# An edge MLP with gather and scatter on one core: transposes a period ahead, chunks scattered in pairs by adding DMAs

## The chip, the cores and the metric

The kernel runs on one core of a Trainium2 chip. The metric is the device time in microseconds of one execution; times given for a kernel are medians over runs. The engines are TensorE (PE; PEld are its weight loads), VectorE (DVE), ScalarE (ACT), GpSimd (POOL) and SyncE (SP, which issues DMAs).

## The reference

A message-passing layer on a graph of 12,500 nodes and 800,000 edges. Each edge takes the features of its two ends (64 each) and its own attributes (16), multiplies them by `w_msg` (144 x 64), and passes the result through SiLU. The messages are summed over the edges that end at each node, and each node is updated.

```python
N, deg, D, De = 12500, 64, 64, 16          # E = N * deg = 800000, src and dst random
m_in  = jnp.concatenate([x[src], x[dst], e_attr], axis=-1)
msg   = silu(m_in @ w_msg)
agg   = segment_sum(msg, dst, N)
out   = silu(jnp.concatenate([x, agg], axis=-1) @ w_upd)
```

## The kernel before

**Two halves that run at the same time.** The first half sorts edges by destination; the second computes messages from the sorted edges. Nodes are cut into 128 buckets of 98. The product with `w_msg` is split: `A_d` in memory holds each node's part for `src`, and `BW` on chip holds, for each bucket, the part for `dst` and the rows for the attributes.

*Sorting, by steps.* A step takes 8 tiles of 128 edges (782 steps in all). `Step.onehot` (ACT) writes each edge's bucket as a one-hot row `hf`; `sums` (DVE) and `count` (PE, into `z`) count how many edges of the same bucket stand before each edge; `ranks` (DVE) reduces that to a rank; `expand` (DVE) compares the ranks with a ramp (`ioS`, held in PSUM) to get `hit`, and multiplies the edges' records (16 attributes and one packed index, `R` = 17 floats) into their slots, `X`; `move` (PE) multiplies `hf` by `X`, so that in `pl` each bucket (a partition) gets its records side by side. What is collected before it is written out is a *chunk*: 8 tiles for the first 140 steps, 12 tiles after that. So in the first stage every step ends a chunk, and after that three steps end two. `end.blk` (ACT) copies a chunk out of PSUM, `place` (DVE) works out where each bucket's records go in the store `st` in memory, and `scatter` (POOL) is an indirect DMA with one row for each bucket: up to 30 records of 68 B, 2040 B. A record that does not fit in its chunk's limit is noted in `LOST` and handled at the end.

*Messages, by batches.* The store is read back in tiles of 128 records of one bucket. A `Group` (up to 64 tiles) forms over several periods: it works out on DVE and PE which buckets have whole tiles ready, and SP loads those tiles into `rt`. Groups take units of 1 tile first (`FIRST`), then of 2, then of 4 tiles (`QU`). A `Batch` is 6 or 8 tiles of a group. `gather` (POOL) issues one indirect DMA a tile, which fetches 128 rows of `A_d` (256 B each); `onehot` (DVE, ACT) builds `q`, the one-hot of the node within the bucket beside the attributes; `transpose(0)` (PE) and `transpose(1)` (ACT) turn it into `qt`; `product` (PE) multiplies by `BW`, into `pre`; `message` adds the gathered rows (DVE) and applies SiLU (ACT); `reduce` (PE) multiplies by the one-hot and sums by node, into `ag`; `add` (DVE) adds that to `ACC`.

**The order of the work.** It is written out by hand in `period`. One period carries a step in three stages (`h`, then `z`, then `p`) and a batch in four (`q`, `t`, `a`, `r`), each one period behind the one before. Every engine executes in the order in which `period` issues. Before the change PE's order within a period is: `count` of z, `transpose` of t, `reduce` of r, `move(0)` of p, `product` of t, `move(1)` of p. (`move(1)` is the second part of a step in which one 12-tile chunk ends and the next begins.) POOL's order is: half of the batch's gathers, the scatter of the chunk that ended a period earlier, the other half. A batch's first gather also waits for the reduction of the batch four earlier, whose buffer it reuses.

**The planner.** `step` decides before each period whether a new group may start. It does not know the data: `Draws` draws 16 sets of Poisson counts, and a group starts when its units would be there in all 16, with 6 to spare. Stages follow one another: a stage of larger units begins when the stage before has taken its total.

**PSUM tiles** come from pools of one buffer each: `z`, `cb` (constants), `pl`, `t` (transposes), `pre` and `ag`; the small matmuls of a forming group use `ag` too.

**After the last step** come the remaining batches, the last partial tiles and the node update.

Of the kernel before, what the change touches and what calls it, by code (L numbers as in the profile page):

```python
# [3 lines left out]
F32 = mybir.dt.float32  # L4
# [25 lines left out]
XR = 2 + W  # L30
# [6 lines left out]
FIRST = [(1, 48, BT, (1, 0, 1, 0)), (2, 24, 6, (3, 3, 2, 2))]  # L37
# [7 lines left out]
SUMMED = "the sum that this reads waits for the gathers into its buffer, the older ones there were read ahead of them"  # L45
LISTED = "the work list holds buckets and tiles of the store"


def mpnn_kernel(tc, x, e_attr, src, dst, w_msg, w_upd, out):
# [7 lines left out]
    CAPT = (K8 * S8 + (NCH - K8) * S) // P + 2  # L57
# [3 lines left out]
    NREC = TOP * P  # L61
# [11 lines left out]
    with es:  # L73
# [4 lines left out]
        pz = pool("pz", 1, space=PSUM)  # L78
        pc = pool("pc", 1, space=PSUM)
        pp = pool("pp", 1, space=PSUM)  # L80
        pt = pool("pt", 1, space=PSUM)
        ppre = pool("ppre", 1, space=PSUM)
        pag = pool("pag", 1, space=PSUM)

        A_d = dr.tile([NB * BK, D], F32, name="A_d")
        XU_d = dr.tile([BK, NBK * D], F32, name="XU_d")
        st = dr.tile([NREC, R], F32, name="st")
        st_t = st.rearrange("(t e) c -> t (e c)", e=P)

# [32 lines left out]
        cb = pc.tile([P, 512], F32, name="cb")  # L122
        ioB = cb[:, 0:BK]
        ioS = cb[:, BK:BK + S]
        hit = cb[:, P:P + M * S].rearrange("p (k s) -> p k s", s=S)
# [3 lines left out]
        nc.vector.tensor_scalar(out=ioS, in0=iof[:, 0:S], scalar1=RK, scalar2=None, op0=OP.add)  # L129

# [7 lines left out]
        ub = {u: cp.tile([NBK, 1], F32, name=f"ub{u}") for u in (1, 2, QU)}  # L138
        nc.vector.tensor_scalar(out=ub[1], in0=ipf, scalar1=float(CAPT), scalar2=None, op0=OP.mult)
        ptr0 = cp.tile([NBK, 1], I32, name="ptr0")  # L140
        nc.vector.tensor_scalar(out=ptr0, in0=ub[1], scalar1=float(P), scalar2=None, op0=OP.mult)
# [3 lines left out]
        capm = cp.tile([NBK, 2 + len(FIRST)], F32, name="capm")  # L145
# [8 lines left out]
        stages = []  # L154
        for i, (u, gt, bt, give) in enumerate(FIRST):
# [7 lines left out]
            stages.append(dict(u=u, gt=gt, bt=bt, cap=cap, caps=caps, total=u * sum(caps)))  # L163
        stages.append(dict(u=QU, gt=GT, bt=BT, cap=None, caps=None, total=None))
# [5 lines left out]
        class Nodes:  # L170
# [20 lines left out]
            def turn(t):  # L191

                xt_p = pt.tile([P, BT * P], F32, name="xt_p", tag="t")
# [9 lines left out]
            def parts(t, i):  # L203
                ps = (ppre, pag)[i % 2].tile([P, 512], F32, name="abp", tag=("pre", "ag")[i % 2])
# [8 lines left out]
        def tables():  # L213
# [3 lines left out]
            for i in range(-3, len(ts) + 2):  # L217
                if at(i):
                    at(i).turn()
# [117 lines left out]
        ACCf = ACC.rearrange("p b k -> p (b k)")  # L337
        for t in X:
            nc.gpsimd.memset(t[:, :, 0:1], 1.0)
        nc.gpsimd.memset(sent, 0.0)  # L340
# [6 lines left out]
        def later():  # L347
# [5 lines left out]
            if len(zeros) == 15:  # L353
                for k in range(P // SR):
# [7 lines left out]
        bp = pool("bp", 2)  # L362
        sm = pool("sm", 4)
        rcp = pool("rcp", 2)
# [6 lines left out]
        state = dict(x=0, rt=0, u=1, ptr=ptr0, done=done0, stage=0, taken=0, straight=True)  # L371

        blocks = []
        gathers = []
        live = []

        prior = dict(step=None, pl=None)

        class Step:


            def __init__(c, hi, rec, index, n=M):

                c.hi, c.rec, c.n = hi, rec, n
# [4 lines left out]

                c.last = {k: K8 + (index * M + k) // c.size for k in range(n) if c.pos[k] == c.size - 1}  # L390
# [27 lines left out]
            def count(c):  # L418

                hb = c.hf.bitcast(BF16).rearrange("p m (b two) -> p m b two", two=2)[:, :, :, 1]  # L420
                c.z = pz.tile([P, M, NBK], F32, name="z")
# [13 lines left out]
            def expand(c, rs=None):  # L435
# [6 lines left out]
                nc.vector.tensor_tensor(out=c.x[:, :, 1], in0=rank, in1=limc[:, c.turn, :], op=OP.is_ge)  # L442
                nc.vector.tensor_tensor(out=hit, in0=ioS[:, None, :].to_broadcast([P, M, S]), in1=rank[:, :, None].to_broadcast([P, M, S]), op=OP.is_equal)
                for k in range(0, c.n, 2):
                    n = LIM[c.pos[k]]
                    nc.vector.tensor_tensor(out=c.x[:, k:k + 2, 2:2 + n * R].rearrange("p k (s c) -> p k s c", c=R), in0=hit[:, k:k + 2, 0:n, None].to_broadcast([P, 2, n, R]),  # L446
                                            in1=c.rec[:, k:k + 2, None, :].to_broadcast([P, 2, n, R]), op=OP.mult)

            def move(c, part=None):
# [4 lines left out]
                for k in reversed(range(c.n)) if whole else range(c.n):  # L454
# [3 lines left out]
                    if n == (c.size - 1 if whole else 0):  # L458
                        prior["pl"] = pp.tile([P, 512], F32, name="pl")
                    pl = prior["pl"]  # L460
                    w = 2 + LIM[n] * R
                    ends = n == (0 if whole else c.size - 1)
                    nc.tensor.matmul(pl[:, 0:w], c.hf[:, k, :], c.x[:, k, 0:w], start=(n == (c.size - 1 if whole else 0)), stop=ends, skip_group_check=True)  # L463
                    if ends:
                        w = 2 + LIM[c.size - 1] * R
                        end = Chunk(*c.last.values())
                        end.blk = bp.tile([NBK, XR], F32, name="blk")[:, 0:w]
                        nc.scalar.activation(end.blk, pl[:, 0:w], AF.Copy)  # L468
                return end

        class Chunk:


            def __init__(c, index):
                c.index, c.m = index, M if index < K8 else min(C, NT - K8 * M - (index - K8) * C)

            def place(c, ptr_new):

                c.ptr, b = state["ptr"], c.blk
                lost = LOST[:, c.index:c.index + 1]  # L480
                nc.vector.scalar_tensor_tensor(out=lost, in0=b[:, 1:2], scalar=0.0, in1=b[:, 0:1], op0=OP.is_gt, op1=OP.mult)
                nc.vector.scalar_tensor_tensor(out=ptr_new, in0=b[:, 0:1], scalar=lost, in1=c.ptr, op0=OP.subtract, op1=OP.add)
                state["ptr"] = ptr_new

            def scatter(c):
                i = nc.gpsimd.indirect_dma_start(out=st, out_offset=bass.IndirectOffsetOnAxis(ap=c.ptr, axis=0), in_=c.blk[:, 2:], in_offset=None)  # L486
                tc.declare_no_dep(i.ins, group="units", reason=WHOLE)
                blocks.append(i.ins)

        def regs(row, u, n, engine, top):  # L490
            return nc.values_load_multi_w_load_instructions(row[0:1, u:u + n], engines=(engine,), min_val=0, max_val=top, skip_runtime_bounds_check_because=LISTED)[1]

        class Group:


            def __init__(g, u, ptr, done_old, done_new, ceil, gt=GT, base=None, cap=None, bt=BT):
                g.u, g.ptr, g.done_old, g.done_new, g.ceil, g.gt = u, ptr, done_old, done_new, ceil, gt
                g.base = ub[u] if base is None else base
                g.b0, g.cap = None, cap
                g.gu, g.bt = gt // u, bt  # L500
                g.quick = cap is not None
                g.nl = NL[u]
# [32 lines left out]
            def fourth(g):  # L535
                k = g.k
                gu = g.gu
                if k == 0:
                    urec = g.u * P
                    c = (urec - 1) / (2.0 * urec) * (1.0 if g.ceil else -1.0)  # L540
# [8 lines left out]
                    nc.vector.scalar_tensor_tensor(out=new, in0=v, scalar=-MAGIC, in1=g.done_old, op0=OP.add, op1=OP.subtract)  # L549
                    nc.vector.tensor_tensor(out=t1, in0=g.base, in1=g.done_old, op=OP.add)  # L550
# [26 lines left out]
            def middle(g):  # L577
# [4 lines left out]
                elif g.k == 1:  # L582
                    cbc, mat = g.wl[7], g.mat
                    g.ps = pag.tile([P, 512], F32, name="ps2", tag="ag")
# [10 lines left out]
        class Last(Group):  # L595


            def __init__(g, b0, n):
                super().__init__(1, ptrg, None, None, False, n)
# [11 lines left out]
            def middle(g):  # L611
                if g.k == 1:
                    g.ps = pag.tile([P, 512], F32, name="ps3", tag="ag")
# [6 lines left out]
        class Batch:  # L620
# [41 lines left out]
            def transpose(t, step):  # L662
                w = t.n * P
                if step == 0:
                    t.grp.over = t.i0 + t.n >= t.grp.gt
                    t.tq = pt.tile([P, BT * P], F32, name="tq", tag="t")
                    for j in range(t.n):
                        nc.tensor.transpose(t.tq[0:KQ, j * P:(j + 1) * P], t.q[:, j, :], ident)  # L668
                else:
                    t.qt = qtp.tile([KQ, BT * P], F32, name="qt")  # L670
                    nc.scalar.activation(t.qt[:, 0:w], t.tq[0:KQ, 0:w], AF.Copy)  # L671

            def product(t):
                t.pre = ppre.tile([P, 512], F32, name="pre")
# [16 lines left out]
            def reduce(t):  # L691
                t.ag = pag.tile([P, 512], F32, name="ag")
                u = t.grp.u
                for j in range(0, t.n // u, 2):
                    for k in range(u):
                        for v in range(j, min(j + 2, t.n // u)):
                            i = v * u + k
                            o = nc.tensor.matmul(t.ag[t.half(v), v // 2 * BK:(v // 2 + 1) * BK], t.g[:, i, :], t.q[:, i, 0:BK], start=(k == 0), stop=(k == u - 1))  # L698
                            t.gathers.append(o.ins)
# [13 lines left out]
        pipe = dict(h=None, z=None, s=None, q=None, t=None, a=None)  # L713

        def period(step=None, batch=None, ptr_new=None):

            h, z, p, s = step, pipe["h"], pipe["z"], pipe["s"]
            q, t, a, r = batch, pipe["q"], pipe["t"], pipe["a"]
            forms = [g for g in work["forming"] if not g.ready()]
            e = None  # L720
            pipe.update(h=h, z=z, q=q, t=t, a=a)
# [15 lines left out]
            for g in quick:  # L737
                g.middle()
                g.k = 1
            if t:  # L740
                t.transpose(0)
                t.weights()
                t.transpose(1)
            if r:
                r.reduce()
            if z:
                z.ranks()
            if a:
                a.message()
            if r:  # L750
                r.add()
# [7 lines left out]
            for g in quick:  # L759
# [427 lines left out]
```

## Time and profile before

| | us |
|---|---|
| median of 3 runs | 8911.29 |
| lowest, highest | 8909.55, 8912.29 |
| span of the profiled execution | 10886.0 |

The profiled execution is one run under the hardware profiler; it is longer than the timed runs. Its times are from the start of its span. In rows of groups the columns are: line, engine, operation, output and input tiles, count; then busy us and mean ns of one; then idle us just before them and what ended that. In rows of a timeline: start us, length us, engine, line, operation, tiles and shape; in brackets the engine's idle time before it and what ended it. `issue` is idle time in which the engine waited for nothing that the profile shows, `remote` is a release that the profile can't name. In rows of stretches: the stretch and its length, then busy us and count of PE, PEld, DVE, ACT and POOL, the granted PE clock as a share of full speed, the share of DMA engines, GB/s.

| stage | us from the start |
|---|---|
| steps alone | 0 to 200 |
| first gather | 200.12 |
| last step's rank | 10036.79 |
| last gather | 10848.35 |

### The profile page before, as it was taken

To read this page: it belongs to the slowest core of one execution; us is meant where nothing else is said; L and a number is where in the kernel's file an instruction comes from. 1 tells how busy PE (TensorE), PEld (TensorE's weight loads), DVE (VectorE), ACT (ScalarE), POOL (GpSimd) and SP (SyncE) were. 2 spreads that over 40 slices of the span, in tenths; PEclk is the share of its full clock that TensorE was granted. 3 is DMA by queue.
4 is the path that set the end of the run, shared out by engine and by line. 5 is a ranking of instruction groups with operands and counts; after the bars stand their busy time and mean duration, and the time that the engine had idled before them with its cause. 6 is when DMAs were issued, how large, how long until landed. Compare 5 with 4: busy or idle time off the path is not lost. (4 is left out here: it accounts for less than half of the span.)

```text
span 10886.0 us, 155616 instructions
## 1 busy us (share of the span) xinstructions
PE 8949.9 (82%) x49053; PEld 6219.2 (57%) x49816; DVE 7231.4 (66%) x15936; ACT 5082.6 (47%) x12594; POOL 6571.4 (60%) x6908
## 2 busy tenths in 40 slices
PE   8788888888888888888888888888888888888556
PEld 5566655555555555555555555555555555555555
DVE  7777776666666666766666666666666666766232
ACT  6455554444444444444444444444444444544211
POOL 2565666666666666666666666666666666666555
PEclk9999998999989988999998999999899998988555
DMA  3111111111111111111111111111111111111212
GB/s 97 44 49 48 49 49 46 43 47 42 47 42 46 45 44 45 44 43 44 46 43 46 44 44 43 46 47 43 45 42 46 43 47 44 44 45 41 46 36 44
DMA packets 662903, 501.15 MB, mean 46 GB/s; under 512 B 492983, under 2 KB 529911, under 8 KB 662071
## 3 DMA queue, kind: packets, MB, share of 16 engines
q0 software_dynamic: 238976, 349.72, 12.3%
q1 hardware_dynamic: 422775, 141.27, 5.9%
q8 instruction: 400, 6.55, 0.3%
q14 instruction: 432, 3.54, 0.1%
q10 hardware_dynamic: 320, 0.07, 0.0%
HBM read 330.05 MB, written 152.30 MB: 44 GB/s over the span
## 5 line engine op out<-in xcount | busy, mean ns | idle before, releaser
L649 POOL DMA_INDIRECT g<-A_d,sidx x6322 | 5997.6, 949 | 3658.7 <-issue 1620.7
L463 PE MATMUL pl<-X,hf 128*128 128x291 f32 (+5 forms) x12512 | 4745.0, 524 | 476.4 <-issue 428.3
L463 PEld LDWEIGHTS pl<-X,hf 128*128 128x128 f32 x12512 | 2538.7, 211 | 2159.4 <-issue 1737.4
L446 DVE TENSOR_TENSOR X<-cb,rec 128x442 f32<-128x442 f32 (+5 forms) x3128 | 2646.6, 908 | 26.7
L396 ACT ACTIVATE hf<-iof,shi 128x128 f32<-128x128 f32 x6256 | 1908.8, 389 | 1360.4 <-PE pl L463 449.0
L671 ACT ACTIVATE qt<-tq 114x1024 f32<-114x1024 f32 (+1 forms) x818 | 811.7, 992 | 2951.3 <-remote 2298.5
L433 DVE TENSOR_REDUCE rank<-z 128x8 f32<-128x1024 f32 x782 | 954.5, 1221 | 1270.3 <-remote 874.9
L677 PEld LDWEIGHTS pre<-w,qt 114*128 114x128 f32 x10496 | 1392.5, 209 | 687.8 <-ACT qt L671 467.1
L677 PE MATMUL pre<-w,qt 114*128 114x64 f32 x10496 | 1395.2, 291 | 345.6 <-ACT qt L671 317.6
L710 DVE TENSOR_TENSOR ACC<-ag,ACC 64x98 f32 x1938 | 496.7, 256 | 1553.3 <-remote 1131.7
L698 PE MATMUL ag<-q,g 128*64 128x98 f32 x12644 | 882.3, 276 | 490.4 <-remote 236.2
L698 PEld LDWEIGHTS ag<-q,g 128*64 128x64 f32 x12644 | 681.6, 151 | 668.8 <-issue 381.7
L668 PE MATMUL tq<-ident,q 128*114 128x128 f32 x6322 | 929.9, 294 | 103.3 <-issue 91.5
L668 PEld LDWEIGHTS tq<-ident,q 128*114 128x114 f32 x6322 | 812.6, 147 | 238.7 <-issue 122.6
L397 ACT ACTIVATE hf<-hf,ones 128x1024 f32<-128x1024 f32 x782 | 898.8, 1149 | 25.4
L486 POOL DMA_INDIRECT st<-blk,ptrs x567 | 567.2, 1000 | 561.4 <-ACT blk L468 272.2
L659 DVE TENSOR_TENSOR q<-cb,lo 128x784 f32<-128x784 f32 (+1 forms) x818 | 768.7, 940 | 96.1 <-PE ag L698 46.3
L468 ACT ACTIVATE blk<-pl 128x512 f32<-128x512 f32 (+1 forms) x568 | 324.9, 572 | 818.2 <-PE pl L463 500.9
L426 PE MATMUL z<-G,onesb 128*128 128x384 bf16 x1564 | 529.8, 339 | 78.9 <-issue 25.2
L682 ACT ACTIVATE g<-g 128x512 f32<-128x512 f32 (+1 forms) x818 | 498.4, 609 | 192.5 <-DVE g L681 111.8
L681 DVE TENSOR_TENSOR g<-pre,g 128x512 f32<-128x512 f32 (+1 forms) x818 | 541.3, 662 | 51.4 <-issue 37.2
L677 PE MATMUL pre<-BW,qt 114*128 (+1 forms) x2148 | 326.3, 314 | 99.0 <-ACT qt L671 64.8
(138 smaller groups left out, 5243.9 us busy)
## 6 DMA issues: line engine op xcount, KB each, us to landing
g<-A_d,sidx POOLq DMA_INDIRECT x6322
ea<-in_e_attr SPq DMA_DIRECT2D x260, 192.0 KB
rt<-st SPq DMA_DIRECT2D x1312, 34.0 KB
st<-blk,ptrs POOLq DMA_INDIRECT x567
rt<-st SPq DMA_DIRECT2D x434, 8.5 KB
nodes<-in_x SPq DMA_DIRECT2D x62, 98.0 KB
ACC<-rt SPq DMA_DIRECT2D x11, 544.0 KB
rt<-st SPq DMA_DIRECT2D x320, 17.0 KB
```

The costliest lines, as they stand in the source:

```text
L396: nc.scalar.activation(c.hf[:, k, :], iof, AF.Square, bias=c.hi[:, k:k + 1])
L397: nc.scalar.activation(c.hf, c.hf, AF.Relu, bias=ones, scale=-1.0)
L433: nc.vector.tensor_reduce(out=c.rank, in_=c.z, axis=AX.X, op=OP.max)
L446: nc.vector.tensor_tensor(out=c.x[:, k:k + 2, 2:2 + n * R].rearrange("p k (s c) -> p k s c", c=R), in0=hit[:, k:k + 2, 0:n, None].to_broad ...
L463: nc.tensor.matmul(pl[:, 0:w], c.hf[:, k, :], c.x[:, k, 0:w], start=(n == (c.size - 1 if whole else 0)), stop=ends, skip_group_check=True)
L486: i = nc.gpsimd.indirect_dma_start(out=st, out_offset=bass.IndirectOffsetOnAxis(ap=c.ptr, axis=0), in_=c.blk[:, 2:], in_offset=None)
L649: j = nc.gpsimd.indirect_dma_start(out=t.g[:, i, :], out_offset=None, in_=A_d, in_offset=bass.IndirectOffsetOnAxis(ap=t.grp.sidx[:, k:k + ...
L659: nc.vector.tensor_tensor(out=t.q[:, 0:n, 0:BK], in0=ioB[:, None, :].to_broadcast([P, n, BK]), in1=t.grp.lo[:, i0:i0 + n, None].to_broadca ...
L668: nc.tensor.transpose(t.tq[0:KQ, j * P:(j + 1) * P], t.q[:, j, :], ident)
L671: nc.scalar.activation(t.qt[:, 0:w], t.tq[0:KQ, 0:w], AF.Copy)
L677: nc.tensor.matmul(t.pre[:, i * D:(i + 1) * D], t.qt[:, i * P:(i + 1) * P], w, start=True, stop=True)
L698: o = nc.tensor.matmul(t.ag[t.half(v), v // 2 * BK:(v // 2 + 1) * BK], t.g[:, i, :], t.q[:, i, 0:BK], start=(k == 0), stop=(k == u - 1))
```

## The change

Five things are changed together.

1. *PSUM tiles are held for good.* They are allocated once and named (`zb`, `tb`, `plb`, `preb`, `agb`, `cb`). Small work lists of forming groups use a free corner of `agb` (`listing`).
2. *Transposes a period ahead.* `transpose(0)` of a batch moves from its second period (t) to the end of its first (q), behind `move(0)`. `message` moves ahead of `ranks`; `reduce` moves behind `move(0)`. PE's order is now: `count`, `move(0)`, `transpose` of q, `reduce`, `product`, `move(1)`. `reduce` gets one more matmul with a single column, after which the batch's buffer counts as read.
3. *A period more for chunks.* A chunk that ended is placed a period later (`e`) and scattered two periods later (`s`).
4. *Shared adding scatters.* In the 12-tile stage two chunks (428 chunks, 214 pairs) share one scatter. The first chunk's records stand at the right end of the first half of `BLK` and the second chunk's at the left end of the second half, so that in memory they follow one another; the rest of the row is zeros, and the DMA adds (`compute_op=OP.add`). Rows are 2 x 30 records, 4080 B. The ramp for right-aligned records, `ioD`, is held in SBUF. The store is filled with zeros beforehand: `fill` issues 271 DMAs on SP over the course of the kernel, each 128 rows of 4080 B from a block of zeros in memory, at least four ahead. `BLK` is one buffer of two halves, where `blk` had two buffers. In the 8-tile stage a scatter still writes one chunk without adding.
5. *Overlapping stages.* The first groups have 12, 12 and 24 tiles of one tile a unit, up to 2, 1, 2, 1 tiles a bucket by quarter (before: 48 tiles, up to 1, 0, 1, 0), in batches of 6 tiles (before: 8). Every stage keeps its own count of what it has taken, and `step` starts a group of the first stage that has enough. The large stage's first groups have 32 tiles instead of 64.

```diff
-FIRST = [(1, 48, BT, (1, 0, 1, 0)), (2, 24, 6, (3, 3, 2, 2))]
+FIRST = [(1, (12, 12, 24), 6, (2, 1, 2, 1)), (2, (24,), 6, (3, 3, 2, 2))]
+LATER = (32, 32, 32, GT)
...
+        def fill():
+            a = (P - S + len(filled) * ROW) * R
+            z = nc.sync.dma_start(st_b[:, a:a + ROW * R], Z_d)
+            filled.append(z.ins)
...
             def expand(c, rs=None):
-                nc.vector.tensor_tensor(out=hit, in0=ioS[:, None, :].to_broadcast([P, M, S]), in1=rank[:, :, None].to_broadcast([P, M, S]), op=OP.is_equal)
+                io = ioD[:, :, None, :].to_broadcast([P, 2, M // 2, S]) if turn else (ioS if c.right[0] else ioD[:, 0, :])[:, None, :].to_broadcast([P, M, S])
+                nc.vector.tensor_tensor(out=wide(hit), in0=io, in1=wide(rank[:, :, None].to_broadcast([P, M, S])), op=OP.is_equal)
...
+            def keep(c, pl, right):
+                if c.main:
+                    nc.scalar.activation(c.cnt[:, c.side, :], pl[:, f:f + 2], AF.Copy)
+                c.blk = BLK[:, c.side, 0:n]
+                nc.scalar.activation(c.blk, pl[:, a:a + n], AF.Copy)
...
             def scatter(c):
-                i = nc.gpsimd.indirect_dma_start(out=st, out_offset=bass.IndirectOffsetOnAxis(ap=c.ptr, axis=0), in_=c.blk[:, 2:], in_offset=None)
+                if c.single:
+                    i = nc.gpsimd.indirect_dma_start(out=st, out_offset=at, in_=c.blk, in_offset=None)
+                else:
+                    i = nc.gpsimd.indirect_dma_start(out=st, out_offset=at, in_=BLK.rearrange("p a w -> p (a w)"), in_offset=None, compute_op=OP.add)
...
             def reduce(t):
-                            o = nc.tensor.matmul(t.ag[t.half(v), v // 2 * BK:(v // 2 + 1) * BK], t.g[:, i, :], t.q[:, i, 0:BK], start=(k == 0), stop=(k == u - 1))
-                            t.gathers.append(o.ins)
+                            nc.tensor.matmul(t.ag[t.half(v), v // 2 * BK:(v // 2 + 1) * BK], t.g[:, i, :], t.q[:, i, 0:BK], start=(k == 0), stop=(k == u - 1))
+                o = nc.tensor.matmul(t.ag[0:t.n, 4 * BK:4 * BK + 1], t.g[:, 0:t.n, 0], ones, start=True, stop=True)
+                t.gathers.append(o.ins)
...
         def period(step=None, batch=None, ptr_new=None):
+            if e:
+                e.place(ptr_new)
             if t:
-                t.transpose(0)
                 t.weights()
                 t.transpose(1)
-            if r:
-                r.reduce()
+            if a:
+                a.message()
             if z:
                 z.ranks()
-            if a:
-                a.message()
-            if r:
-                r.add()
...
             if p:
-                e = p.move(0)
+                end = p.move(0)
+            if q:
+                q.transpose(0)
+            if r:
+                r.reduce()
             if t:
                 t.product()
             if p:
                 p.move(1)
-            if e:
-                e.place(ptr_new)
+            if r:
+                r.add()
...
-            pipe["s"] = e
+            pipe["e"] = end if end and end.whole else None
```

More of the change, by code (lines that the diff above doesn't have):

```diff
@@ L45 @@
 SUMMED = "the sum that this reads waits for the gathers into its buffer, the older ones there were read ahead of them"
+AHEAD = "the zeros are written ahead of the rows that any bucket can have reached; a scatter waits for those that it may reach"
 LISTED = "the work list holds buckets and tiles of the store"
@@ L388, in __init__ @@
                 c.prev, prior["step"] = prior["step"], c
+                c.right = [not main or c.turn == 2 or c.turn == 3 or (c.turn == 1 and k >= C - M) for k in range(M)]
                 c.last = {k: K8 + (index * M + k) // c.size for k in range(n) if c.pos[k] == c.size - 1}
@@ L464, in move @@
                     if ends:
[L465 to L468, printed above, removed]
+                        end = Chunk(*c.last.values(), c.main)
+                        end.keep(pl, c.right[k])
                 return end
         class Chunk:
-            def __init__(c, index):
-                c.index, c.m = index, M if index < K8 else min(C, NT - K8 * M - (index - K8) * C)
@@ L501, in __init__ @@
                 g.quick = cap is not None
+                g.back = state["back"]
                 g.nl = NL[u]
```

358 lines of the change are left out of this document (220 added, 138 removed).

## The prediction

> **What bounds the kernel now.** I read the page first (busy shares and costliest groups), then the clock by stage, then the timeline of GpSimd (POOL) alone, then who waited for whom.
>
> ```profile
> span 10886.0 us, 155616 instructions
> ...
> PE 8949.9 (82%) x49053; PEld 6219.2 (57%) x49816; DVE 7231.4 (66%) x15936; ACT 5082.6 (47%) x12594; POOL 6571.4 (60%) x6908
> ...
> L649 POOL DMA_INDIRECT g<-A_d,sidx x6322 | 5997.6, 949 | 3658.7 <-issue 1620.7
> L486 POOL DMA_INDIRECT st<-blk,ptrs x567 | 567.2, 1000 | 561.4 <-ACT blk L468 272.2
> ```
>
> By busy shares TensorE (PE, 82%) leads and POOL (60%) looks idle. POOL's timeline in the steady stage says otherwise:
>
> ```profile
> 5010.81 0.95 POOL L649 DMA_INDIRECT g<-A_d,sidx  x1 [2.44 <-remote]
> 5012.06 0.94 POOL L649 DMA_INDIRECT g<-A_d,sidx  x1 [0.30 <-issue]
> 5013.30 0.95 POOL L649 DMA_INDIRECT g<-A_d,sidx  x1 [0.31 <-issue]
> 5014.56 0.95 POOL L649 DMA_INDIRECT g<-A_d,sidx  x1 [0.30 <-DMA g<-A_d,sidx]
> 5015.81 1.00 POOL L486 DMA_INDIRECT st<-blk,ptrs  x1 [0.31 <-issue]
> 5017.11 0.96 POOL L649 DMA_INDIRECT g<-A_d,sidx  x1 [0.30 <-issue]
> ...
> 5020.88 0.94 POOL L649 DMA_INDIRECT g<-A_d,sidx  x1 [0.30 <-issue]
> 5024.34 0.95 POOL L649 DMA_INDIRECT g<-A_d,sidx  x1 [2.52 <-DVE g L681]
> ```
>
> Every indirect DMA is followed by 0.30 us in which POOL waits for nothing and still starts nothing. So a gather holds POOL 0.949 + 0.30 = **1.25 us** and a scatter 1.00 + 0.30 = **1.30 us**. All of them: 6322 x 1.25 + 568 x 1.30 = 7903 + 738 = **8641 us** (567 scatters in the row, and the first one, which has a row of its own).
>
> The rest of the profiled span, 10886 - 8641 = 2245 us, is mostly the 2.4 us ahead of each batch's first gather. That gather waits for the reduction of the batch four back. The trace shows why it comes late:
>
> ```profile
> 5005.52 0.38 PE L428 MATMUL z<-G,onesb 128*128 128x512 bf16 x1
> 5006.70 0.90 PE L698 MATMUL ag<-q,g 128*64 128x98 f32 x16
> 5010.14 1.23 DVE L433 TENSOR_REDUCE rank<-z 128x8 f32<-128x1024 f32 x1 [2.60 <-remote]
> ```
>
> PE's records put the end of z at 5005.90 and of the reduction at 5007.60, but the reader of z starts at 5010.14 and POOL's gather at 5010.81. PE's results are seen 3 to 4 us after their recorded end, in each such burst of short matmuls.
>
> The timed runs cannot contain this. Their median is 8911 us, 1975 below the profiled span, and POOL's slots alone take 8641 of it. The remaining 270 us are found at the two ends:
>
> ```profile
> 179.17 0.96 POOL L486 DMA_INDIRECT st<-blk,ptrs  x1 [5.66 <-ACT blk L468]
> 185.79 0.96 POOL L486 DMA_INDIRECT st<-blk,ptrs  x1 [5.66 <-ACT blk L468]
> 200.12 0.97 POOL L649 DMA_INDIRECT g<-A_d,sidx  x1 [13.37 <-DVE sidx L530]
> ...
> 238.44 0.95 POOL L649 DMA_INDIRECT g<-A_d,sidx  x1 [0.30 <-issue]
> 247.62 1.00 POOL L486 DMA_INDIRECT st<-blk,ptrs  x1 [8.23 <-ACT blk L468]
> ...
> 305.87 0.94 POOL L649 DMA_INDIRECT g<-A_d,sidx  x1 [0.30 <-issue]
> 311.27 1.00 POOL L486 DMA_INDIRECT st<-blk,ptrs  x1 [4.46 <-ACT blk L468]
> ...
> 343.56 0.96 POOL L486 DMA_INDIRECT st<-blk,ptrs  x1 [8.02 <-ACT blk L468]
> 355.12 0.98 POOL L649 DMA_INDIRECT g<-A_d,sidx  x1 [10.61 <-PE z L428]
> ...
> 10848.35 0.94 POOL L649 DMA_INDIRECT g<-A_d,sidx  x1 [0.30 <-issue]
> ```
>
> Before the first gather: 200, less 22 scatters of 1.30, is 171. Between the first stage of groups and the second (305.87 to 355.12, less one gather and four scatters): 43. At 238.44: 8. After the last gather: 36. Sum 258 of the 270. So I take it that in the timed runs **POOL's issue of indirect DMAs is the bound**, without a pause from the first group on. The profiled execution shows nothing around its span of 10886; I set the sum against that and against the median, in slots, not by a ratio.
>
> How far off is PE?
>
> ```profile
> L463 PE MATMUL pl<-X,hf x9628: 348/547/1207, 1702.1 to 9700.0; 128*128 128x223 f32 x36, 128*128 128x291 f32 x33, 128*128 128x359 f32 x32, 128*128 128x410 f32 x32
> 500.00:1300.00 800.00, 666.35 (x3726) 487.78 (x3799) 613.93 (x1613) 418.03 (x1028) 481.67 (x503) 0.92 0.20 49
> 1700.00:9700.00 8000.00, 6745.60 (x36911) 4577.32 (x37513) 5492.84 (x11580) 3859.84 (x9629) 4966.48 (x5216) 0.91 0.17 45
> 10100.00:10800.00 700.00, 425.53 (x2524) 372.08 (x2526) 185.68 (x495) 129.05 (x258) 417.93 (x443) 0.56 0.23 40
> ```
>
> The move makes 16 matmul records a step, so 1700 to 9700 holds 9628 / 16 = 602 periods. PE's busy time at the granted clock is 6745.60 x 0.91 / 602 = 10.2 us of full-clock work a period; VectorE (DVE) 9.1, ScalarE (ACT) 6.4. POOL, with eight gathers and two thirds of a scatter: 10.87. PE stands only 0.7 us behind.
>
> **The change, part by part.**
>
> *Shared adding scatters.* The 428 chunks behind the first 140 go out in pairs: 214 scatters fewer, 214 x 1.30 = **-278 us**. Each that is left moves rows of 4080 B instead of 2040 and adds in memory. No row shows an adding DMA. Nearest below: a gather of 256 B rows, 0.949; nearest above: two plain scatters, the work that it replaces, 2.60 with issue. From 256 B to 2040 B the price rises 0.05, so for twice the bytes I add 0.06, **+13 us** (ends -11 and +278). I take the low value because descriptors per row, not bytes, seem to set POOL's time, and their number stays 128.
>
> *Zero fill.* 271 DMAs of 128 rows go from memory to memory on SP's queue ahead of the scatters. SP issues them beside its loads of tiles; the DMA engines are 17% busy in the table above. Behind a fill on SP stand the loads of e_attr and of the next group's tiles, which run periods ahead. Price 0 in the steady stage. At the start the first scatters now wait for zeros, made on ACT, written out and copied: I take **+10 us** (0 to 20, against the 6.62 us between scatters at 179 and 185).
>
> *Overlapping stages, small first groups.* The first group asks for 12 tiles, not 48 of 64 buckets. A bucket gets about 8 records a step, so 12 (and 6 spare) full tiles of 128 exist near step 14.5, 54 near 17.4: three periods earlier. A 12-tile list loads in one period instead of three: two more. Placing a period later takes one back. Four periods of 6.62: **-26 us**. The later stages may start before the first ends, so the pauses of 43 and 8 go: **-51 us**. Batches of six tiles instead of eight (about 9 batches more) add no gathers.
>
> *Transposes ahead, message and reduce reordered, held PSUM tiles.* Product no longer waits within a period for transposes and ACT's copy. Both stand beside POOL's slots, so this is worth nothing while POOL binds; without that cover it is worth PE's waits, at most POOL's 10.87 less 10.2. The reduction now sits behind the first move and the new transposes on PE, so the next batch's first gather, and the seven and the scatter behind it, are released later in PE's period; their data is wanted two periods on, hence 0.
>
> *Closing matmul in reduce.* One 1-column matmul a batch, two records and two loads.
>
> ```profile
> L585 PE MATMUL ps<-mat,wl 128*1 128x16 f32 (+5 forms) x230 | 23.8, 179 | 17.7 <-DVE wl L562 5.9 <-DVE mat L561 4.0 <-remote 3.6
> L585 PEld LDWEIGHTS ps<-mat,wl 128*1 128x1 f32 x230 | 9.9, 81 | 42.0 <-issue 19.1 <-DVE wl L562 7.4 <-DVE mat L561 5.4
> L443 DVE TENSOR_TENSOR cb<-cb,rank 128x240 f32<-128x240 f32 x782 | 324.5, 415 | 3.0
> 5012.43 0.42 DVE L405 TENSOR_TENSOR G<-hf 128x256 bf16<-128x256 f32 x1
> ```
>
> At most 2 x (23.8 + 9.9) / 230 = 0.29 us; in a pipelined run, as the reduction's own 16 records in 0.90, 0.11. PE becomes 10.3 to 10.5 a period and POOL 8 x 1.25 + 1.36 / 3 = 10.45. They meet. For the 642 periods of the paired stage I take the upper end, 0.04 each: **+25 us** (0 to 25).
>
> *Place and keep.* Two more small ACT copies a pair, six small DVE operations instead of four, all beside POOL. But both halves of a pair share one buffer. The copy of the next pair's first half waits until the scatter has read it; behind that copy on ACT stand the next step's one-hots, and PE's second move waits for the freed bank. From POOL's start of that period: five slots (6.3), the landing, the copy (0.6), then PE's own work up to the reduction that frees POOL's same period of the next pair, about two of its 10.2 us periods: 27 plus the landing, against three POOL periods, 31.3. Price 0 while an adding scatter lands within 4 us.
>
> Sum: 8911 - 278 + 13 + 10 - 26 - 51 + 25 = **8604 us**, 3.4% less. Against the profiled execution the same terms give 10886 - 307 = 10579, if the 2.4 us stay.
>
> **Rivals.**
>
> *A, the adding scatter is dear.* If POOL builds twice the descriptors (it must read its target), each costs two plain slots and the saving is gone: 8604 + 278 - 13 = 8869. For it: read, add and write is more work; against: the flat price from 256 B to 2040 B. From 1.30 x 2 + 0.3 = 2.9 us it would end slower. 18 in 100.
>
> *B, slower: PE is the bound in the timed runs too.* Then POOL's fewer slots give nothing, and each of 818 batches pays for the closing matmul: 0.2 x 818 = 164, less the 67 at the start: 9008. It decides from 67 / 818 = 0.08 us a batch. For it: PE's 82%, 10.2 us close behind. Against: the 8641 + 258 that add up to the median. 12 in 100.
>
> *C, the shared buffer binds.* With a landing of 6 us, 2 us a pair: 8604 + 428 = 9030; at 5 us 8820. No row gives the landing of an adding scatter. 7 in 100.
>
> *D, VectorE locks POOL out.* In turns 0 and 1 the 'hit' compare (L443) reads its ramp from SBUF instead of PSUM, so both inputs lie in SBUF. If each held POOL for its 0.415 us, 428 of them cost 178: 8782. Against: the G sum of 5012.43 reads two SBUF inputs, lies across a gather, and that gather took 0.94. The Trainium skill (SBUF — State Buffer, Who interferes with whom) says that a VectorE instruction with two SBUF inputs contends with a GpSimd instruction that reads SBUF, which speaks against this change. By that rule it would be 8782; the trace does not agree for gathers. 5 in 100.
>
> **How the numbers follow.** Forecast 58, A 18, B 12, C 7, D 5 in 100. The likeliest gives 8604, its own range 8540 to 8680 (ends of the terms, and some jitter between PE and POOL now that they meet). To hold 8 in 10 the upper end must reach A: 8500 to 8890. A change under 0.2% (18 us) is about what this measurement cannot tell from none. Faster: 58 + 5, most of A (12) and part of C (3): 78. Same: 4, from A. Slower: B, and the rest of A and C: 18.
>
> **What would show it.** In the profile after: 214 adding scatters of about 1.06 us with 0.30 behind them (right), or 2 us and more (A). First gather near 175 to 185 instead of 200, no pause near 305. POOL again in runs of 1.25 us with one pause a batch. Gathers beside the compare at 0.95 (not D). ACT's copy of the first half waiting for a DMA or POOL would be C. If the time falls far less than POOL's slots do, the reading of POOL as the bound is wrong.

## The result and the profile after

The change makes the kernel slower: 9828.44 us (9827.24 to 9843.33) against 8910.91 (8909.55 to 8912.29), a ratio of 1.1034 [1.1018, 1.1049]. Forecast was 8604. The profile of before in the prediction shows an execution of 10886 us, and one chip met later takes 10868 for that kernel in every run; all kernels below were compared on chips where it takes 8910, except three that are marked.

The page of the changed kernel:

```profile
span 9825.4 us, 162309 instructions
...
PE 8600.8 (88%) x51528; PEld 6128.8 (62%) x51528; DVE 7362.0 (75%) x17005; ACT 5108.1 (52%) x13146; POOL 6564.7 (67%) x6696
```

Its gathers and its adding scatters on POOL (busy us and mean ns, then the idle time ahead of them):

```profile
L740 POOL DMA_INDIRECT g<-A_d,sidx x6322 | 6064.7, 959 | 2956.3 <-issue 1772.1 <-PE ag L790 947.3 <-DMA g<-A_d,sidx 125.7
L569 POOL DMA_INDIRECT st<-BLK,cnt x214 | 351.9, 1644 | 65.2 <-issue 53.6 <-ACT cnt L539 6.7 <-DMA g<-A_d,sidx 1.5
```

Two things are new. POOL's gathers now wait 947 us for the closing matmul of the reduction (L790). And an adding scatter takes 1.644 us, not the 1.06 that was forecast. The waits (us in total, times, longest) tell where the first comes from:

```profile
ACT BLK L541 <- DMA st<-BLK,cnt: 1497.0, 212, 11.7
POOL g L740 <- PE ag L790: 947.3, 255, 8.8
PE pl L515 <- ACT BLK L541: 896.8, 224, 9.2
```

Taken in the order first, third, second, these rows are one chain. ACT's copy into BLK waits for the adding scatter that still reads BLK, 212 times, once for nearly each of the 214 pairs; PE's second move waits for that copy, because it writes the bank that the copy empties; POOL's gathers wait for the reduction that stands behind the move on PE. The timeline shows it for one pair:

```profile
5025.34 1.63 POOL L569 DMA_INDIRECT st<-BLK,cnt  x1 [0.30 <-ACT cnt L539]
5027.27 0.97 POOL L740 DMA_INDIRECT g<-A_d,sidx  x1 [0.30 <-issue]
...
5031.54 0.60 ACT L541 ACTIVATE BLK<-pl 128x510 f32<-128x510 f32 x1 [6.34 <-DMA st<-BLK,cnt]
5032.19 3.55 PE L515 MATMUL pl<-X,hf 128*128 128x223 f32 x8 [3.44 <-ACT BLK L541]
...
5036.57 6.01 PE L515 MATMUL pl<-X,hf 128*128 128x359 f32 x16
...
5044.21 0.20 PE L790 MATMUL ag<-ones,g 128*8 128x1 f32 x2
5044.68 0.94 POOL L740 DMA_INDIRECT g<-A_d,sidx  x1 [2.68 <-PE ag L790]
```

POOL is done with the scatter at 5026.97, but ACT's copy starts at 5031.54. The packets agree: the last of a scatter's 128 packets of 4080 B ends 4.4 us after POOL's end (median; 4.1 to 7.6 for nine in ten), where a plain scatter's last packet ends 1.4 us after. The Trainium skill (Perfetto Trace Analysis, DMA Instruction — SWDGE (GPSIMD)) says that GpSimd's interval ends with the last descriptor written, not with the data moved; these packets agree.

The stall costs more than its length, as the clock shows (last columns: granted clock, DMA share, GB/s). In the pair ahead of this one PE had waited 5.2 us, up to 4996.60:

```profile
4995.00:5000.00 5.00, 3.40 (x8) 2.67 (x9) 0.00 (x0) 0.60 (x1) 3.78 (x5) 0.50 0.22 53
5000.00:5005.00 5.00, 5.00 (x16) 2.63 (x15) 2.08 (x3) 4.54 (x13) 3.33 (x4) 0.88 0.16 27
5005.00:5010.00 5.00, 5.00 (x38) 3.23 (x37) 4.13 (x9) 3.56 (x11) 0.21 (x1) 1.00 0.02 4
```

After the wait PE runs at half its clock until 5001.2, for 4.6 us. The Trainium skill (TensorE: Matmul & The Clock Gate, What's actually happening) has the clock fall to half after an idle window of about 3.4 us; these rows, with a wait of 5.2 us, agree.

### The profile page after: what moved, and what is told of

Its sections match the earlier page's. It is cut to its first block, busy times and chain, and to the rows that moved or that the text cites. A ratio compares the mean times of both kernels' runs of the same rounds, so it can differ in the third digit from the quotient of the medians.

```text
span 9825.4 us, 162309 instructions
## 1 busy us (share of the span) xinstructions
PE 8600.8 (88%) x51528; PEld 6128.8 (62%) x51528; DVE 7362.0 (75%) x17005; ACT 5108.1 (52%) x13146; POOL 6564.7 (67%) x6696
## 3 DMA queue, kind: packets, MB, share of 16 engines
q0 software_dynamic: 242400, 349.71, 19.6%
## 5 line engine op out<-in xcount | busy, mean ns | idle before, releaser
L740 POOL DMA_INDIRECT g<-A_d,sidx x6322 | 6064.7, 959 | 2956.3 <-issue 1772.1
L515 PE MATMUL pl<-X,hf 128*128 128x291 f32 (+5 forms) x12512 | 4420.2, 508 | 897.3 <-ACT BLK L541 896.8
L767 PE MATMUL pre<-w,qt 114*128 114x64 f32 x10176 | 1289.9, 281 | 3.1 <-DVE g L771 3.1
L767 PEld LDWEIGHTS pre<-w,qt 114*128 114x128 f32 x10176 | 1202.5, 194 | 18.1 <-DVE g L771 3.3
L541 ACT ACTIVATE BLK<-pl 128x510 f32<-128x510 f32 (+1 forms) x568 | 325.3, 573 | 1635.2 <-DMA st<-BLK,cnt 1497.0
L757 PE MATMUL tq<-ident,q 128*114 128x128 f32 x6322 | 875.5, 283 | 120.0 <-ACT qt L761 90.4
L788 PE MATMUL ag<-q,g 128*64 128x98 f32 x12644 | 776.7, 264 | 1.3 <-DVE lgi L1163 1.3
L788 PEld LDWEIGHTS ag<-q,g 128*64 128x64 f32 x12644 | 611.0, 143 | 156.8 <-issue 124.4
L471 PE MATMUL z<-hf,w 128*128 128x512 bf16 x1564 | 666.9, 426 | 0.0
L539 ACT ACTIVATE cnt<-pl 128x2 f32<-128x2 f32 x568 | 97.4, 171 | 924.2 <-PE pl L515 919.6
```

Of the source, the lines that this page charges most:

```text
L471: nc.tensor.matmul(c.z[:, k:k + ZB, :], w1, hb[:, k:k + ZB, :], start=True, stop=False)
L515: nc.tensor.matmul(pl[:, a - o:b - o], c.hf[:, k, :], c.x[:, k, a:b], start=(n == (c.size - 1 if whole else 0)), stop=ends, skip_group_che ...
L740: j = nc.gpsimd.indirect_dma_start(out=t.g[:, i, :], out_offset=None, in_=A_d, in_offset=bass.IndirectOffsetOnAxis(ap=t.grp.sidx[:, k:k + ...
L757: nc.tensor.transpose(tb[0:KQ, j * P:(j + 1) * P], t.q[:, j, :], ident)
L767: nc.tensor.matmul(t.pre[:, i * D:(i + 1) * D], t.qt[:, i * P:(i + 1) * P], w, start=True, stop=True)
```

## Experiments

Theory W: the one BLK buffer, held until the adding scatter has landed, is the whole loss. Rival X: the new order on PE with its closing matmul, or the added DMA traffic, is.

### Two buffers

```diff
-        BLK = lp.tile([NBK, 2, W], F32, name="BLK")
+        BLKS = [lp.tile([NBK, 2, W], F32, name=f"BLK{i}") for i in range(2)]
...
+                c.buf = BLKS[(index // 2 if c.single or not main else (index - K8) // 2) % 2]
-        RT = [lp.tile([P, GT, R], F32, name=f"rt{i}") for i in range(4)]
+        RT = [lp.tile([P, GT, R], F32, name=f"rt{i}") for i in range(3)]
```

> The changed kernel with two BLK buffers used in turn (one of the four tile buffers rt is given up for the space). Theory W (the wait on the shared buffer): in the paired stage three periods take 36.3 us, POOL's slots in them 24 x 1.25 + 1.93 = 31.9 and PE's work 31.3; the ACT copy of a pair's first half waits 7.06 us for the scatter before. With a second buffer that wait is gone and POOL sets the time: 9828 - 214 x (36.3 - 32.0) = 8908, between 8820 and 9000. Rival X (the adding scatters and zero fills load the DMA engines, or the added matmul and the new order on PE cost the time): the wait goes but the time stays above 9500.

Measured: 8892.36, ratio 0.9978 [0.9968, 0.9988]. The loss of 10% is gone, with the closing matmul, the order on PE and the fills all kept. The copy's wait for the scatter, 1497 us in the changed kernel, no longer stands among the waits of this run. Its groups on POOL:

```profile
L741 POOL DMA_INDIRECT g<-A_d,sidx x6322 | 6051.5, 957 | 2043.2 <-issue 1683.1 <-DMA g<-A_d,sidx 190.2 <-PE ag L791 74.6
L570 POOL DMA_INDIRECT st<-BLK,cnt x214 | 351.6, 1643 | 65.2 <-issue 44.5 <-ACT g L773 5.2 <-ACT G L449 4.6
```

POOL's idle time ahead of gathers falls by 913 us, the span by 928. So W holds. The fourth record buffer had to go for the space; the control keeps one BLK and drops that buffer as well:

> Control for e1_two_buffers, which had to give up one of the four buffers of record tiles (RT) for the space of the second BLK: the changed kernel with three of them and its one BLK. Theory W (the one BLK and the landing of the adding scatter are the loss): 9830 (9780 to 9890), as changed. Rival: the later loads of record tiles are what helped e1_two_buffers: 8900 to 9500.

Measured: 9812.38, 1.1012 [1.0993, 1.103]. The record buffers are not what helped.

### The scatter ahead of the period's gathers

```diff
-            if q:
-                q.gather(0, BT // 2)
             if s:
                 s.scatter()
             if q:
-                q.gather(BT // 2, BT)
+                q.gather(0, BT)
```

> The changed kernel, with the scatter issued ahead of all gathers of its period instead of behind the first four: 5 us earlier, with nothing else moved and one buffer as before. Theory W: the 7.06 us wait of the copy shrinks to about 2, PE's stall of 4.2 us a pair goes, 8900 to 9050. Rival X: no change, 9750 to 9850.

Measured: 8950.83, 1.0046 [1.003, 1.0063], with one BLK as in the changed kernel. The waits:

```profile
ACT BLK L541 <- DMA st<-BLK,cnt: 854.4, 209, 9.9
PE pl L515 <- ACT BLK L541: 304.3, 156, 7.0
POOL g L740 <- PE ag L790: 94.0, 60, 7.5
```

Four slots earlier on POOL, 5 us, and the chain breaks at its second link: ACT still waits 4 us a pair, PE 1.4, POOL's gathers 0.4. The wait on ACT costs only what it pushes through to POOL.

### One buffer in the kernel before

```diff
-        bp = pool("bp", 2)
+        bp = pool("bp", 1)
```

> The kernel before with one buffer for blk instead of two in turn, plain scatters of 2040 B rows as they were. Here the copy of a chunk waits for the scatter of the chunk ahead of it, which lands about 1.5 us after POOL's end. Theory W (a shared buffer costs nothing by itself; what costs is a landing that comes after PE's and ACT's turn): before, a scatter goes out in the period in which its chunk was copied, so there are 5 us or more left: 8910 to 8960. Rival, one buffer costs in any case, whatever the scatter: 9100 to 9900.

Measured: 8933.15, 1.0027 [1.0017, 1.0036]. The waits:

```profile
ACT blk L468 <- DMA st<-blk,ptrs: 1593.9, 209, 12.0
PE pl L463 <- ACT blk L468: 319.0, 152, 4.1
POOL g L649 <- PE ag L698: 13.8, 45, 0.3
```

ACT waits more than in the changed kernel, 1594 us against 1497, and POOL not at all. So a single buffer does not cost by itself. It costs with the landing of the adding scatter, 3 us later, in a loop that has no such time to spare. That the later landing is what tips this loop is read from the loop's legs (below); no run changes the landing with everything else as it is.

### What the add costs

Dropping the add makes the paired scatter a plain one of 4080 B rows.

```diff
-..., in_offset=None, compute_op=OP.add)
+..., in_offset=None)
```

> The changed kernel with the paired scatter writing instead of adding (so zeros of a row overwrite records of its neighbours: the sums leave these out; number and size of all instructions stay). What the adding itself costs: POOL's slot should go from 1.93 to about 1.35 and the landing from 4.4 us to some 2.5. Theory W: the wait shortens by about 2.5 us and POOL's part by 0.6 for each of 214 pairs: 9100 to 9400. If the adding were harmless: 9750 or more. If the adding were all of it: under 9000.

Measured: 9483.37, 1.0648 [1.063, 1.0666]. Its scatters and its software-made packets (share of 16 engines' span):

```profile
L569 POOL DMA_INDIRECT st<-BLK,cnt x214 | 217.1, 1015 | 77.8 <-issue 45.4 <-DVE X L499 13.6 <-ACT cnt L539 8.5
```

```profile
q0 software_dynamic: 228704, 349.71, 45.0%
```

Twice the row costs 0.015 us, less than the 0.06 of the prediction; the add itself costs 1.644 - 1.015 = 0.63 us on POOL. The time is above the 9100 to 9400 that were expected. Those packets take 45% of the engines' time, the same bytes in the changed kernel 19.6%, and the median gather packet 455 ns against 133. One reading is that the overwritten records all point to the same node rows; that was not tried. The scatter's last packet here ends 3.6 us after POOL's end (median), so the landing is disturbed too, and this run prices only what the add costs on POOL.

Without any sharing (a plain scatter a chunk, no fills, the rest of the change kept):

```diff
-                c.right = [not main or c.turn == 2 or ... for k in range(M)]
+                c.right = [True] * M
...
-                c.single = index < K8
+                c.single = index < K8 or main
```

> The changed kernel without sharing: each chunk has its own plain scatter, the halves of BLK are used in turn, there is no zero fill, records are left-aligned. Everything else of the change stays (held PSUM tiles, transposes ahead, reduce behind the move, closing matmul, a period more for chunks, overlapping stages). Theory W: POOL's 26 slots a pair, 32.6 us, set the time; against before only the start is gained: 8850 to 8990. Rival X in its second form (the new order or the closing matmul cost the time): above 9400.

Measured: 8998.55, 1.0101 [1.0084, 1.0118], a little above the range: even so the rest of the change costs 89 us. Against b0_before_again (below) the trace has 63 us more of POOL's gaps behind the first gather, 15 more behind the last, and 12 more in the gathers; the first gather comes 21 us earlier, but five scatters that stood ahead of it now stand behind it.

### Is POOL the bound before the change?

> The kernel before, unchanged, for a profile of an execution as long as the timed ones (the profile in the prediction is of one 1975 us longer). If POOL's slots bind it, as the prediction reads it: span 8905 to 8915, POOL's indirect DMAs one behind the other at 1.25 and 1.30 us from 1700 on, gaps beyond the 0.30 us of under 60 us between 1700 and 8500, period 10.8 to 10.9 us. Rival, PE binds it too: the same span, but a gap of 0.5 us or more ahead of the first gather of most batches, 300 us and more in that stretch, with the reduction's L698 as the releaser.

Measured: 8907.9. The groups and the stretch from 1700 us on:

```profile
L649 POOL DMA_INDIRECT g<-A_d,sidx x6322 | 6008.6, 950 | 1949.1 <-issue 1514.7 <-DMA g<-A_d,sidx 266.4 <-PE ag L698 34.8
L486 POOL DMA_INDIRECT st<-blk,ptrs x567 | 566.6, 999 | 314.6 <-issue 156.3 <-ACT nodes L196 99.2 <-ACT blk L468 28.0
```

```profile
1700.00:8500.00 6800.00, 6363.66 (x38575) 4487.95 (x38572) 5575.24 (x11761) 3892.73 (x9723) 5145.85 (x5404) 0.95 0.23 54
```

Of 1949 us, 6322 slots of 0.305 make 1928. From 1500 to 8500 POOL has 8 us of further gaps in 5562 instructions. And with one gather more a batch:

```diff
                     t.gathers.append(j.ins)
+                    if i == t.n - 1:
+                        nc.gpsimd.indirect_dma_start(out=GX, out_offset=None, in_=A_d, in_offset=bass.IndirectOffsetOnAxis(ap=t.grp.sidx[:, k:k + 1], axis=0))
```

> The kernel before with one gather more a batch, into a tile that nobody reads (818 gathers more, 128 rows of 256 B each; no other engine has more to do). If POOL's slots bind the kernel before in its timed runs: 8910 + 818 x 1.25 = 9930 (9880 to 9990). Rival, PE binds it and POOL has 0.7 us a period to spare or more: 8910 to 9400.

Measured: 9926.4, 1.1144 [1.1125, 1.1162]; 9930 was expected. Each gather added costs its whole slot. POOL is the bound, though PE is busy for 92% of the span.

### Where the rest of the gain went

With the loss taken away, POOL binds on both sides, and yet the gain is 0.2% and not 3.4%. The next kernels have the two remedies together (e8, f2), and then other first groups as well:

```diff
-FIRST = [(1, (12, 12, 24), 6, (2, 1, 2, 1)), (2, (24,), 6, (3, 3, 2, 2))]
-LATER = (32, 32, 32, GT)
+FIRST = [(1, (16, 16, 24), BT, (2, 1, 2, 1)), (2, (24,), BT, (3, 3, 2, 2))]    # e9, f3
+FIRST = [(1, (48,), BT, (1, 0, 1, 0)), (2, (24,), 6, (3, 3, 2, 2))]            # e11, f4
-LATER = (32, 32, 32, GT)
+LATER = (GT,)                                                                  # e11, f4
```

> The two remedies together: two BLK buffers in turn (e1_two_buffers) and the scatter ahead of the period's gathers (e6_scatter_first). POOL is the bound in e1_two_buffers, and only 24 us of gaps are left between 1500 and 8500 us, so the order of the scatter can give back at most these: 8870 (8855 to 8895). Rival: the scatter first delays the gathers that a batch waits for, so a batch comes later: 8900 to 8950.

> e8_two_buffers_scatter_first with eight tiles a batch in the first groups instead of six, and 16, 16, 24 tiles in them instead of 12, 12, 24. In e1_two_buffers POOL has 81 us of gaps before 1500 us, most behind the late reduction; the kernel before, with batches of eight, has 26. If PE is the bound where a period has only six gathers (6 x 1.26 + 1.31 = 8.9 us on POOL against about 10 on PE), 40 to 55 us come back: 8820 (8800 to 8850). Rival: the gaps come from the later start of a list, not from the size of a batch: 8860 to 8890, as e8.

> e8_two_buffers_scatter_first with the first groups of the kernel before: 48 of 64 tiles in batches of eight, then 24 in batches of six, all later groups of 64. The first gather comes about 6 us later than in e8, and the gaps before 1500 us fall from 81 to about 26 if they come with the changed first groups: 8825 (8810 to 8850). Rival: the gaps come with the order of the message and the reduction, not with the groups: 8870 to 8900.

These three ran on a chip on which the kernel before takes 10868, so the expectations don't apply: 10613.97 (0.9763 [0.9746, 0.978]), 10921.52 (1.0046 [1.0032, 1.0059]) and 10648.7 (0.9793 [0.978, 0.9807]). POOL is not the bound there: between 1500 and 8500 us it has gaps of 1166 us in e8, and over the whole run its gathers wait 976 us for the closing matmul and 782 for what the profile calls remote, as in the profile of the prediction. Again, on another chip:

> e1_two_buffers again, beside the three below on one chip. Where the kernel before takes 8910: 8892 (8880 to 8900). Where it takes 10868, as beside e8_two_buffers_scatter_first: about 10620, as e8 there.

> e8_two_buffers_scatter_first again. Where the kernel before takes 8910, POOL is the bound and 24 us of gaps are left between 1500 and 8500 us: 8870 (8855 to 8895). Rival: the scatter first delays the gathers that a batch waits for: 8900 to 8950. Where the kernel before takes 10868: 10614.

> e9_eight_a_batch again. Where the kernel before takes 8910: if POOL's gaps before 1500 us come from batches of six, 40 to 55 us under f2. Rival: PE's longer period in the first stages (eight product matmuls more in a batch) makes them anyway: within 15 us of f2, or above it, as on the other chip, where it was 308 us above.

> e11_first_groups_as_before again. On the other chip its first gather came at 229.1 instead of 192.3 and 23 scatters stood before it instead of 18. Where the kernel before takes 8910: 30 us later at the start, less 5 scatters of 1.30, and up to 55 us fewer gaps before 1500: 8870 less 30, within 8820 to 8890. Rival, the groups do not matter for the gaps: 8895 to 8910.

Measured: f1 8891.76 (0.9981 [0.9972, 0.999]), f2 8892.11 (0.9979 [0.997, 0.9988]), f3 9008.11 (1.0109 [1.0094, 1.0125]), f4 8861.45 (0.9942 [0.9929, 0.9956]).

f2 equals f1: once the buffer is free, the scatter's place gives nothing, and the forecast 24 us were not to be had. f3 goes to its rival, and further: with larger batches and larger lists, which this run changes together, it is worse by 116, with 138 us of gaps before 1500 against 82 in f2. So larger batches do not take f2's gaps away. f4 beats both kernels. Its groups:

```profile
L741 POOL DMA_INDIRECT g<-A_d,sidx x6322 | 6045.2, 956 | 1966.1 <-issue 1670.3 <-DMA g<-A_d,sidx 140.4 <-PE ag L791 22.6
L570 POOL DMA_INDIRECT st<-BLK,cnt x214 | 348.4, 1628 | 65.2 <-issue 56.4 <-ACT hf L443 4.6 <-ACT hf L442 2.7
L568 POOL DMA_INDIRECT st<-BLK,ptrs x139 | 138.3, 995 | 202.7 <-DVE G L451 117.9 <-ACT BLK L542 31.2 <-issue 23.8
```

Its first gather comes at 231.7, f2's at 193.6, and still it ends 31 us sooner: POOL's gaps after the first gather are 51 us instead of 109. So the changed first groups and list sizes as a whole are a loss. Which of their parts (sizes of the lists, the number of tiles taken, the start of a group) makes the gaps stays open.

## Why the prediction was wrong

**The step that failed: "Price 0 while an adding scatter lands within 4 us".** It put the wait on the shared buffer at nothing. Rival C named the right mechanism and the right wait, with 7 in 100; the threshold and the price beyond it were wrong. The prediction's loop ran from POOL's start of the period through five slots (6.3, the scatter's among them), the landing, the copy and two PE periods (21.0): 27 plus the landing. Over 186 pairs between 1700 and 8500 us, the means of its legs in the trace are: start of the scatter to the copy of the next pair's first half 7.3, copy to the gather that it releases 13.9, that gather to the next scatter 15.2. Sum 36.4, the measured distance of two scatters. Against the prediction the leg through ACT and PE is 7 us shorter, but POOL's part, 15.2 and 1.6 for the scatter, is 10.5 longer: the released gather does not stand four slots ahead of the scatter but about twelve, since it opens the period before.

Three periods of POOL's own work, 24 gathers and an adding scatter, take 32.2 us in e1_two_buffers (mean distance of two scatters in the same stretch). With the other legs as measured, the copy had to start 32.2 - 15.2 - 13.9 - 1.6 = 1.5 us after POOL's end. It started 5.7 us after it (mean; the last packet lands at 4.4 in the median, 5.2 in the mean), and (36.4 - 32.2) x 214 = 899 is most of the 936 that e1_two_buffers gave back. The formula for C, the landing less 4, gives 0.4 to 1.7 us a pair for such a landing; measured are 4.2. They also hold PE's half clock after the stall. Its share was not measured by itself; the views from 1700 to 8500 give a granted clock of 0.92 here and 0.96 in e1_two_buffers, so an estimate is 0.04 x 36.4, some 1.5 us a pair at most.

**Shared adding scatters: mis-sized.** Forecast 1.36 a slot; measured 1.64 + 0.305 = 1.95 (the groups of e1_two_buffers). 214 such slots less 428 plain ones of 1.305 is -142, not -265: 123 us less saved. The choice of the low end rested on the reading that bytes hardly matter, which e3_plain_pair bears out; the add is what costs. Rival A, at 2.9 a slot, overshot.

**First groups and pauses: wrong sign.** Forecast -77; f4 against f2 puts the changed groups at +31, 108 us off. The first gather does come earlier: at 179 instead of 200 in e2_no_sharing, which has no fills (26 us were forecast), and with the fills at 194 in e1_two_buffers. But half of the pauses of 43 and 8 taken for gains lay only in the execution of 10886 us: behind the first gather, b0_before_again has 26 us of gaps before 1500. And the changed groups make pauses of their own, 84 us before 1500 in f1, mostly behind the reduction on PE (75 us of waits). The prediction looked at what the new groups start sooner, not at what PE can feed in those periods.

**Start, gathers and tail: missed.** With the first groups of before, f4's first gather comes 31 us later than in b0_before_again, of which 10 were forecast and 1.3 are one scatter more ahead of it: 20. The fills are some 4 of these (below); the later placing is a likely part of the rest, which no run shows by itself. 957 ns a gather in e1_two_buffers against 950 makes 43 us; 34 us after the last gather instead of 20 makes 14. The closing matmul cost nothing to be seen (below): -25. Together 123 + 108 + 20 + 43 + 14 - 25 = 283, of the 288 from 8604 to the 8892 of e1_two_buffers.

**Right.** POOL as the bound, almost without a pause (b0_before_again, e5_more_gathers), which refutes rival B. Zero fills: the first gather comes 14 us later in e1_two_buffers than in e2_no_sharing, inside the 0 to 20 forecast. Closing matmul and fills in the steady stage: f4 keeps both and has 7 us of gaps from 1500 to 8500, where b0_before_again has 8, so the matmul is at the lower end of 0 to 25. Transposes and order at 0 there, once the buffer is out of the way; none of them was taken back by itself. Rival D may exist in small (below): at most the 43 us by which the gathers grew, not 178, and not for its compare alone. In e2_no_sharing the compare reads its ramp from PSUM, and 216 gathers are still over 1.05 us, against 305 in e1_two_buffers and 112 in b0_before_again. The one gather that the prediction read was one of the many that stay short.

## What to carry to other kernels

Where two stages share a buffer, write down the whole closed loop, with the landing of the transfer (not the end of its issue) and every queue that it passes, and compare it with the period of the bound engine. As read from these runs, a wait on an engine off the bound costs next to nothing until it is longer than the reserve of each engine that it passes, and then what is over, here with a lower clock besides. The total of a wait does not tell which (1594 us in e10_before_one_buffer cost 23, 1497 in the changed kernel cost 936). Where a profile is longer than the timed runs, take from it durations of single instructions, not pauses.

## What was not expected of the hardware

An indirect scatter that adds takes 1.64 us on POOL where a plain one of the same rows takes 1.015. Its last packet ends 4.4 us after that, where it is 1.4 for the plain scatter of 2040 B rows in b0_before_again.

Some gathers are longer when VectorE works beside them. In b0_before_again, of 4822 gathers that have nothing of the G sums and the two compares beside them, none took more than 1.05 us; of 760 with over 0.8 us of these beside them, 15 in 100 did. No run changes VectorE's work alone, so that VectorE holds them up is argued and not shown. In e1_two_buffers 305 gathers take more than 1.05 us, for instance:

```profile
467.81 0.42 DVE L451 TENSOR_TENSOR G<-G,hf 128x256 bf16<-128x256 bf16 x1
467.89 1.16 POOL L741 DMA_INDIRECT g<-A_d,sidx  x1 [0.30 <-issue]
468.27 0.29 DVE L458 TENSOR_TENSOR G<-G,hf 128x128 bf16<-128x128 bf16 x1
468.48 0.17 DVE L491 TENSOR_TENSOR X<-rank,limc 128x8 f32<-128x8 f32 x1
468.56 0.41 DVE L494 TENSOR_TENSOR cb<-cb,rank 128x240 f32<-128x240 f32 x1
```

The same five instructions 18 us later leave a gather at 0.95. It may depend on the moment within the gather; which moment was not settled.

The same kernel takes 8910 us on some chips and 10868 on another, with the granted clock at 0.94 in the profiled execution of 8906 and 0.885 in that of 10886. One and the same edit (e8 and f2) is worth 2.4% on the latter and 0.2% on the former.
